# dV outer products that read 32 rows, 31 of them zero, in place of one row

## Chip, cores, metric

One core of one Trainium2 chip. The metric is the device time of one execution in microseconds. "Faster" or "slower" is said of a change of more than 2%. All runs told here are fast runs; for one core that means that no run lay over 1.5% above the fastest of its kernel.

## The reference

A decode block with its backward pass. What matters here is attention with one query per head: 32 heads, 8192 keys, head size 192, all in bf16. For each head the gradient of V is an outer product of the softmax row with the gradient of the attention output, the gradient of K one of dS with the query:

```python
scores = jnp.einsum('bhqd,bhkd->bhqk', q, k) * Dh ** (-0.5)   # q has one row
p = _softmax(scores, axis=-1)
o = jnp.einsum('bhqk,bhkd->bhqd', p, v)
# ... projection, MLP, and then jax.vjp of all of it:
# dV[k, :] = p[k] * dO[:],   dP[k] = V[k, :] . dO,   dK[k, :] = dS[k] * q[:]
```

Reading K and V and writing dK and dV is nearly all of the traffic: 342 MB read and 226 MB written.

## The kernel before

The forward half takes up to about 555 us. The backward half walks 64 steps, two per head. Each step reads one V tile of 128x6144 and writes one tile of dV and one of dK. dV is made on TensorE: for every block of keys an outer product of one row of the transposed softmax (`er`) and one row of dO. The er rows lie on partitions 0, 32, 64 and 96, and two such products, which read different blocks of rows, run side by side: the second of a pair starts 5 ns after the first (median in the trace before). ScalarE copies the result from PSUM.

```python
er_b = [bst.tile([P, R8, P], BF16, name=f"er_b{k}") for k in range(2)]
# ...
def load_er(s):
    er = er_b[s % 2]
    # ...
    nc.gpsimd.dma_start(out=er[0:P:32, :, :], in_=er_t[0][r0 : r0 + JH, :])

def mul_q(s, q):     # VectorE: V * dO, half a tile
    V_.tensor_tensor(out=pq[:, q], in0=v_l[s][...], in1=do_of(ht(s)[0])..., op=ALU.mult)

def tree_q(ps, q, lo=0, hi=DH):   # TensorE adds up the columns of it: dP
    for k in range(lo, hi, TS):
        T_.matmul(ps[:, q * JQ : (q + 1) * JQ, :], lhsT=ident_bf, rhs=pq[:, q, :, k : k + TS], ...)

def dv_groups(dV, er, doh, gs):
    for g in gs:
        m, q = divmod(g, 2)
        ps = psV.tile([P, 2, 512], FP32, name="dv_ps", tag="v")
        for k in range(2):
            for b in range(2):
                p0 = 32 * (2 * q + b)
                T_.matmul(ps[:, b, k * DH : (k + 1) * DH], lhsT=er[p0 : p0 + 1, 2 * m + k, :],
                          rhs=doh[p0 : p0 + 1, :], start=True, stop=True)
        A_.copy(out=dV4[...], in_=ps[:, :, 0:PW])
```

dO (`doh`) stands in all 128 partitions alike. The step loop mixes `mul_q`, `tree_q`, dV groups, dK products (VectorE), weight-gradient work and loads and stores (cut here). The stores and the small er loads go through one DMA queue, that of GpSimd; the V loads through SyncE's.

## Time and profile before

| | before |
|---|---|
| time, median of 3 | 1443.19 us |
| span of the profiled run | 1440.5 us |
| mean granted TensorE clock, whole / from 612 to 1384 us | 0.72 / 0.56 |
| DMA rate, 612 to 972 / 972 to 1384 us | 418 / 394 GB/s |
| one backward step, mean of steps 0 to 29 / 30 to 58 | 13.2 / 13.7 us |

The granted clock is the share of full speed that the clock records of the trace give TensorE. In the trace before these are 52 records; they hold only 0.5 and 1.0 and change only at the edges of windows of 3.413 us. A window at half clock is called cold here, one at full clock warm. A step is counted from one dP reduction on VectorE to the next. The views are read as in the prediction below: slices for where the clock is, stretches for what each half is bound by, the chain for who carries it.

### The profile page before, as it was taken

The numbers are of one execution on the slowest core, as the hardware profiler recorded it, in microseconds if no ns is written. First come the engines' busy times: TensorE is split into PE (matmuls) and PEld (weight loads), VectorE is DVE, ScalarE is ACT, GpSimd is POOL, SyncE is SP. The second block draws the span as 40 slices with busy tenths as digits, with TensorE's granted clock in tenths as the row PEclk, the third lists the DMA queues.
The fourth block names the chain that finished last, engine by engine and source line by source line (L and its number), as shares of the span: only waits on it lengthen the run. The fifth ranks groups of instructions, "written<-read, shape, count | busy, mean of one in ns | idle before, by whom it ended". The sixth has DMA issues, their size and how long they took to land.

```text
span 1440.5 us, 29990 instructions
## 1 busy us (share of the span) xinstructions
PE 1190.4 (83%) x12577; PEld 779.5 (54%) x12577; DVE 1110.3 (77%) x1396; ACT 879.3 (61%) x1920; POOL 138.6 (10%) x240
## 2 busy tenths in 40 slices
PE   3999999999999998876878788878878778778784
PEld 1677777777777677533444444444444444444442
DVE  4999999999999997776667667766667667666773
ACT  0777777677777763545656566655565556555653
POOL 0000000000000000212111111111111111111111
PEclk7999999999999997765555555555555555555655
DMA  9999999999999994699999999999999999999998
GB/s 375 401 420 418 418 415 417 401 416 407 414 411 413 418 399 176 249 413 416 424 422 417 409 420 419 417 419 413 370 425 394 417 376 407 382 398 404 382 363 364
DMA packets 77764, 570.39 MB, mean 396 GB/s; under 512 B 8606, under 2 KB 26734, under 8 KB 37566
## 3 DMA queue, kind: packets, MB, share of 16 engines
q1 hardware_dynamic: 51418, 342.02, 58.7%
q0 software_dynamic: 26192, 226.47, 38.3%
q8 instruction: 98, 1.61, 0.4%
q14 instruction: 36, 0.29, 0.0%
q10 hardware_dynamic: 20, 0.00, 0.0%
HBM read 342.00 MB, written 225.91 MB: 394 GB/s over the span
## 4 chain that ended last, share of the span: by engine, by line
PE 42%; DVE 28%; DMA 12%; issue 8%; ACT 7%; POOL 1%; SPq 0%; ACTq 0%; POOLq 0%; DVEq 0%
PE dot_ps L970 19%; DMA KB<-in_A_k_cache_dram 9%; DVE prod L303 8%; PE dv_ps L981 7%; DVE pq L961 6%; DVE prod L308 4%; PE wT_ps L857 4%; PE mp L386 4%; PE dot_ps L314 3%; DVE vs L364 2%; PE mp L391 2%; ACT wT L858 2%; ACT KB L982 2%; DMA out_dram<-KB 2%; DMA out_dram<-stg 1%
## 5 line engine op out<-in xcount | busy, mean ns | idle before, releaser
L982 ACT CAST KB<-dv_ps 128x768 bf16<-128x768 f32 x504 | 382.3, 803 | 281.6 <-PE dv_ps L981 280.7
L970 PE MATMUL dot_ps<-pq,ident_bf 128*128 128x256 bf16 x1536 | 357.7, 402 | 76.8 <-DVE pq L961 76.6
L371 ACT ACTIVATE vs<-VB,Ef 128x192 bf16<-128x192 bf16 x840 | 303.2, 443 | 0.0
L970 PEld LDWEIGHTS <-ident_bf 128*128 128x128 bf16 x1536 | 187.9, 133 | 201.5 <-issue 141.8
L981 PE MATMUL dv_ps<-do_r,er_b 1*128 1x192 bf16 x2048 | 220.2, 333 | 55.2 <-ACT KB L982 54.9
L303 DVE TENSOR_TENSOR prod<-KB,qs_bc 128x6144 bf16<-128x6144 bf16 x62 | 207.9, 3353 | 21.1 <-DMA KB<-in_A_k_cache_dram 14.0
L986 DVE TENSOR_TENSOR KB<-qs_bc,dS 128x3072 bf16<-128x3072 bf16 x126 | 220.5, 1750 | 0.1
L961 DVE TENSOR_TENSOR pq<-VB,do_r 128x3072 bf16<-128x3072 bf16 x126 | 220.5, 1750 | 0.0
L981 PEld LDWEIGHTS <-er_b 1*128 1x128 bf16 x2048 | 92.7, 111 | 173.8 <-issue 170.5
L386 PE MATMUL mp<-vs,KB 128*128 128x193 bf16 x1920 | 185.2, 249 | 0.0
L386 PEld LDWEIGHTS <-KB 128*128 128x128 bf16 x1920 | 165.4, 98 | 18.5 <-issue 6.5
L318 DVE TENSOR_REDUCE dP<-dot_ps 128x32 f32<-128x512 f32 x64 | 44.2, 691 | 149.3 <-PE dot_ps L970 149.3
L838 POOL DMA_DIRECT2D er_b<-er_t x64 | 40.9, 640 | 1144.4 <-DVE ln_xc L755 554.0
L314 PE MATMUL dot_ps<-prod,ident_bf 128*128 128x512 bf16 x372 | 96.5, 398 | 46.9 <-DVE prod L308 46.7
L364 DVE TENSOR_TENSOR vs<-VB,E 128x1728 bf16<-128x1728 bf16 x120 | 123.6, 1051 | 0.0
L308 DVE TENSOR_TENSOR prod<-prod 128x3072 bf16<-128x3072 bf16 x62 | 108.7, 1754 | 1.0
L858 ACT COPY wT<-wT_ps 128x1024 bf16<-128x1024 bf16 x84 | 80.8, 962 | 42.9 <-PE wT_ps L857 42.8
L391 PE MATMUL mp<-vs,KB 128*64 128x193 bf16 x1920 | 103.4, 251 | 0.0
L391 PEld LDWEIGHTS <-KB 128*64 128x64 bf16 x1920 | 77.3, 110 | 19.6 <-issue 19.6
L314 PEld LDWEIGHTS <-ident_bf 128*128 128x128 bf16 x372 | 38.0, 107 | 85.6 <-issue 58.3
L351 ACT ACTIVATE E<-S_h,negm 128x256 bf16<-128x256 f32 x30 | 15.2, 508 | 109.1 <-DVE negm L528 109.1
L1229 POOL DMA_DIRECT2D out_dram<-KB x127 | 68.8, 546 | 32.5 <-ACT KB L982 17.5
(338 smaller groups left out, 1011.9 us busy)
## 6 DMA issues: line engine op xcount, KB each, us to landing
out_dram<-KB POOLq DMA_DIRECT2D x125, 1536.0 KB, 12.0
VB<-in_A_v_cache_dram SPq DMA_DIRECT2D x124, 1536.0 KB, 11.3
KB<-in_A_k_cache_dram SPq DMA_DIRECT2D x63, 1536.0 KB, 12.0
wo_st<-in_A_wo_dram SPq DMA_DIRECT2D x30, 480.0 KB, 11.9
w_st<-in_A_wq_dram SPq DMA_DIRECT2D x12, 960.0 KB, 10.2
out_dram<-stg POOLq DMA_DIRECT2D x8, 960.0 KB, 14.2
out_dram<-wo_st POOLq DMA_DIRECT2D x16, 480.0 KB, 17.9
out_dram<-w_st POOLq DMA_DIRECT2D x7, 960.0 KB, 13.3
```

What stands on the lines that cost most here:

```text
L303: V_.tensor_tensor(out=prod, in0=src, in1=vec[:, None, :].to_broadcast([P, JH, DH]), op=ALU.mult)
L308: V_.tensor_tensor(out=prod[:, :, 0:w], in0=prod[:, :, 0:w], in1=prod[:, :, w : 2 * w], op=ALU.add)
L314: T_.matmul(ps, lhsT=ident_bf, rhs=prod[:, :, k : k + TS], start=(k == 0), stop=(k == w - TS))
L364: V_.tensor_tensor(out=vs[:, 0:n, 0:DH].rearrange("p j (a b) -> p j a b", b=4), in0=v[:, v0 : v0 + n, :].rearrange("p j (a b) -> p j a b", ...
L371: A_.activation(out=vs[:, k, 0:DH], in_=v[:, v0 + k, :], func=ACT.Copy, scale=Ef[:, j0 + k : j0 + k + 1])
L386: T_.matmul(mp[:, 0:MW], lhsT=kb[:, j0 + k, 0:P], rhs=vs[:, k, 0:MW], start=(q == 0 and k == 0), stop=(z and k == JQ - 1), skip_group_chec ...
L391: T_.matmul(mp[p0 : p0 + 64, MO : MO + MW], lhsT=kb[:, j0 + k, P:DH], rhs=vs[:, k, 0:MW], start=False, stop=(z and k >= JQ - 2), skip_grou ...
L961: V_.tensor_tensor(out=pq[:, q], in0=v_l[s][:, q * JQ : (q + 1) * JQ, :], in1=do_of(ht(s)[0])[:, None, :].to_broadcast([P, JQ, DH]), op=AL ...
L970: T_.matmul(ps[:, q * JQ : (q + 1) * JQ, :], lhsT=ident_bf, rhs=pq[:, q, :, k : k + TS], start=(k == 0), stop=(k == DH - TS), skip_group_c ...
L981: T_.matmul(ps[:, b, k * DH : (k + 1) * DH], lhsT=er[p0 : p0 + 1, 2 * m + k, :], rhs=doh[p0 : p0 + 1, :], start=True, stop=True)
L982: A_.copy(out=dV4[:, 2 * q : 2 * q + 2, m * PW : (m + 1) * PW], in_=ps[:, :, 0:PW])
L986: V_.tensor_tensor(out=dK[:, lo:hi, :].rearrange("p j (a b) -> p j a b", b=4), in0=qh.rearrange("p (a b) -> p a b", b=4)[:, None, :, :].to ...
```

## The change

Its intent is to let each dV product read a whole block of 32 rows. The block's other 31 er rows are made zero once, so the result stays the same; the loads only ever write partitions 0, 32, 64 and 96.

```diff
     er_b = [bst.tile([P, R8, P], BF16, name=f"er_b{k}") for k in range(2)]
+    for er in er_b:
+        nc.gpsimd.memset(er, 0.0)
...
-                    T_.matmul(..., lhsT=er[p0 : p0 + 1, 2 * m + k, :], rhs=doh[p0 : p0 + 1, :], ...)
+                    T_.matmul(..., lhsT=er[p0 : p0 + 32, 2 * m + k, :], rhs=doh[p0 : p0 + 32, :], ...)
```

## The prediction

> **What bounds the kernel now.** I read the page's first two parts first (span, busy time, the 40 slices), then the costliest groups, then the table of stretches for the second half, the chain of waits in it, and last the clock in stretches of 3.41 us.
>
> ```profile
> span 1440.5 us, 29990 instructions
> PE 1190.4 (83%) x12577; PEld 779.5 (54%) x12577; DVE 1110.3 (77%) x1396; ACT 879.3 (61%) x1920; POOL 138.6 (10%) x240
> PEclk7999999999999997765555555555555555555655
> DMA  9999999999999994699999999999999999999998
> ```
>
> The kernel has two halves. Up to about 555 us (forward) TensorE runs at its full clock. From about 576 us (backward: dV outer products, dP dot products, dK products) the granted clock is half with short exceptions, although TensorE is busy some 80% of the time there. The change touches only the backward half. What binds there is seen by cutting it in two (columns after the window: PE, PEld, DVE, ACT, POOL busy, clock, DMA share, GB/s):
>
> ```profile
> 612.00:972.00 360.00, 284.88 (x2140) 162.33 (x2137) 246.36 (x339) 210.54 (x305) 58.37 (x100) 0.58 1.01 418
> 972.00:1404.00 432.00, 349.90 (x2585) 197.32 (x2584) 294.93 (x416) 247.90 (x354) 65.64 (x111) 0.54 0.98 394
> ```
>
> The first stretch moves 418 GB/s, as much as the forward half does at its best (420 in the slices): transfers bind it. The second moves 394, so something else holds it back there. The chain of waits inside 972 to 1404 us names it:
>
> ```profile
> by line: PE dot_ps L970 36.4%; PE dv_ps L981 12.9%; DVE pq L961 11.7%; PE wT_ps L857 8.1%; issue 7.0%; ACT KB L982 3.4%; ACT wT L858 3.2%; DMA out_dram<-KB 2.4%; DVE dP L318 1.7%; ACT v_bc L1064 1.7%; DVE dq_junk L1097 1.5%; PE do_ps L871 1
> ```
>
> TensorE carries at least 57% of it (36.4 + 12.9 + 8.1), at half clock. So the late part is bound by a cold TensorE, with the transfers close behind: if it ran at 418 GB/s it would take 432 x 394/418 = 407 us. 25 us is about all that a faster TensorE can win there.
>
> The groups that matter:
>
> ```profile
> L970 PE MATMUL dot_ps<-pq,ident_bf 128*128 128x256 bf16 x1536 | 357.7, 402 | 76.8 <-DVE pq L961 76.6
> L981 PE MATMUL dv_ps<-do_r,er_b 1*128 1x192 bf16 x2048 | 220.2, 333 | 55.2 <-ACT KB L982 54.9
> ```
>
> [...]its clock records are only 0.5 and 1.0, and between 26 us and the end every change falls on a multiple of 3.413 us. [...]at 128 columns the shortest one-row load took 90 ns, the shortest 128-row load 95 ns. [...]the median one-row matmul here took 343 ns.[...]
>
> **How this trace says activity is counted.** The next two tables are the same six windows on the clock's own grid: all work, then the dV products alone (PE busy, ACT busy, clock, DMA share, GB/s).
>
> ```profile
> 879.13:882.54 3.41, 3.41 (x23) 1.69 (x21) 3.41 (x4) 0.91 (x2) 0.00 (x0) 0.50 1.01 413
> 882.54:885.96 3.42, 3.42 (x26) 2.18 (x23) 1.63 (x1) 2.84 (x4) 0.00 (x0) 0.50 1.00 419
> 885.96:889.37 3.41, 1.88 (x21) 1.20 (x20) 2.86 (x4) 2.39 (x5) 1.36 (x3) 1.00 1.00 409
> 892.78:896.20 3.42, 3.42 (x24) 1.62 (x22) 3.35 (x8) 1.37 (x3) 0.00 (x0) 0.50 0.97 402
> 896.20:899.61 3.41, 3.41 (x22) 1.71 (x20) 0.82 (x7) 2.07 (x3) 0.00 (x0) 0.50 1.02 432
> 899.61:903.02 3.41, 2.05 (x31) 1.26 (x28) 3.38 (x4) 3.15 (x5) 0.64 (x1) 1.00 1.03 437
> ```
>
> ```profile
> 879.13:882.54 3.41, 1.16 (x12) 0.91 (x2) 0.50 1.01 413
> 882.54:885.96 3.42, 0.67 (x8) 1.92 (x3) 0.50 1.00 419
> 892.78:896.20 3.42, 1.27 (x12) 1.37 (x3) 0.50 0.97 402
> 896.20:899.61 3.41, 0.76 (x10) 2.07 (x3) 0.50 1.02 432
> ```
>
> TensorE is busy all of the windows at 879, 882, 892 and 896. The two with 0.67 and 0.76 us of dV are followed by the full clock, the two with 1.16 and 1.27 us are not. So one-row products fill time without counting. I then did this for all windows: each matmul counts columns/clock x rows/128 x output columns/128, put 0.1 us after its start (the shift that sorted best). With the dV products at 1/128, in effect nothing, a cold window is followed by the full clock if the sum is at least 0.75 of the window: 228 of 231 obey. A warm window keeps the clock from about 0.36 on: 178 of 179 obey. If a one-row product counted as its whole block of 32 rows, 13 cold and 2 warm windows would disobey. And transposes, whose moving operand is the identity and so is almost all zeros, must count in full (3 disobey; 10 if they count nothing). So zeros count and rows count, as far as this trace can tell.
>
> **The change part by part.** (a) 2048 dV matmuls and their loads read 32 rows. [...]the four row blocks, the number of instructions and every engine's order stay as they were (compared instruction by instruction, only the memsets are new). Cost 0. (b) Two memsets of 128x1024 bf16 on GpSimd. The trace has 128x128 f32 in 0.20 us; eight times that is an estimate of 1.6 us each, 3.2 us. They stand ahead of the first er loads, issued at 555.67 us, whose first reader starts at 575.7; these loads landed in 1.8 to 12.8 us, which leaves slack. GpSimd idles before. Cost 0, at most 1 us. (c) The activity: each dV product now counts 32/128. Counted over the windows after 612 us, 55 of 209 cold ones reach 0.75 where 20 do now; after 972 us, 29 of 123. Of 26 warm windows 8 rather than 7 hold.
>
> What that makes of the late part: 432 us are 127 windows. Chance to rise 29/123 = 0.24, to fall about 0.65 (18 of 26 is 0.69, a little better with the higher count): share warm 0.24/(0.24 + 0.65) = 0.27, or 34 windows, where the mean clock 0.54 says 10 now. That is 24 more. I take two thirds, 16, because a warm window empties TensorE's backlog and makes the next ones thinner. The value of one: over the 29 steps of the backward loop from 981 to 1378 us, the step's length fitted against its number of transposes and its warm windows falls by 0.85 us per warm window (an estimate from scattered steps, residual 1.1 us); for the steps from 657 to 981 us it falls by 0.06, that is nothing, as a transfer-bound stretch should. So 16 x 0.85 = 14 us late, 0 early. The start of the backward half (576 to 612 us, 247 GB/s, clock 0.74) and the tail after 1404 may give 1 us each. Sum: 16 us, to 1427.
>
> **Rivals.** (i) The monitor counts switching data, or blocks of rows, not the rows read: then nothing changes but the memsets, 1443 to 1445. For it: I know only one-row and many-row cases; against it: the transposes and the 13 disobeying windows. I give it 0.2. (ii) The clock rises and hands everything to the transfers: the late part reaches 418 GB/s, 25 us won, 1418, or a few more with start and tail (1412). For it: many cold windows lie between 0.6 and 0.75; against it: a warm window does the same work in half the time, so its sum falls below the 0.36 that holds it (before: 0.20 at 899.61 us). The clock will go up and down, not stay. (iii) Vector and Scalar engine become the bound: DVE is busy 295 of 432 us and ACT 248 late, and product, tree and sum of one step follow each other; this is within the measured 0.85 us. (iv) Slower: memsets delaying the first loads[...]; nothing in the trace shows either.
>
> **Range and chances.** 0.8 x 1427 + 0.2 x 1443 is 1430; I say 1429, range 1415 to 1443.5: the lower end is the late part at full transfer rate plus a little, the upper end the change doing nothing. Faster by over 2% needs less than 1414.3, more than the transfers leave: 0.08. Slower by over 2%: 0.01.
>
> **What would show it.** In the changed profile: dV matmuls listed with 32 rows at 330 to 345 ns when cold; PEclk after 612 us up from about 0.55 to 0.60 to 0.68; windows full of dV products and trees followed by the full clock; 612 to 972 us still at about 418 GB/s and as long as before; the late part at 400 to 412 GB/s. It is wrong if the clock stays at 0.55 (rival i), if it goes above 0.75 (rival ii, hold misjudged), or if it rises and the time does not fall, which would mean that the late part waits for something else than TensorE.

Where cuts are marked, statements of the hardware were taken out that no trace of this case shows. The paragraph ahead of "How this trace says activity is counted" is measured in the trace before ("its" there means that trace). The zero of part (a): the rows read do not change a matmul's time. The traces show it: at 192 columns the cold median in the trace before is 362 ns with one row (dv_ps) and 364 ns with 128 (do_ps), the warm one 241 and 245 ns, and with 32 rows in the changed trace it is 362 and 241 ns. The profile models the ends of matmuls, so by starts alone: a group of four dV products takes 0.433 us cold up to the start of the next matmul in both traces (medians). The sum: 14 us late, 0 early, 1 us each for start and tail, 16 us in all, to 1427. "Monitor", here and in the expectations below, is a name for whatever sets the clock records; the traces show only the records. "Half the time" and the "columns/clock" of the count are in the traces as the distance between the starts of dP products of 256 columns that follow each other: 213 ns cold and 109 ns warm, 0.42 ns per column at full clock. The emptied backlog is seen in the warm windows at 885 and 899 us: 1.88 and 2.05 us of TensorE in 3.41.

## The result

1420.17 us, median of 4 runs (1417.97 to 1423.84), against 1442.90 us for the kernel before on the same chip. The ratio is 0.984, 95% interval 0.981 to 0.987. A ratio is the mean time of one kernel's fast runs over the mean of the other's fast runs of the same rounds, so it is not quite the ratio of the medians. In two later groups on the chip the same kernel gave 0.987 and 0.986. So the change wins 1.3 to 1.6%, within the 2% band, 18 to 23 us.

The page of the changed kernel (span, busy time, slices):

```profile
span 1421.7 us, 29995 instructions
PE 1125.7 (79%) x12577; PEld 747.1 (53%) x12577; DVE 1111.8 (78%) x1396; ACT 876.5 (62%) x1920; POOL 141.0 (10%) x242
PEclk9999999999999997756576657767666667676755
DMA  9999999999999995599999999999999999999998
```

The clock row from slice 18 on has 5s, 6s and 7s where it had almost only 5s. TensorE is busy 65 us less with the same 12577 matmuls. The costliest groups that answer to those of before:

```profile
L972 PE MATMUL dot_ps<-pq,ident_bf 128*128 128x256 bf16 x1536 | 332.9, 380 | 95.0 <-DVE pq L963 94.5
L983 PE MATMUL dv_ps<-do_r,er_b 32*128 32x192 bf16 x2048 | 200.7, 306 | 60.7 <-ACT KB L984 58.6
```

The dV products read 32 rows (32*128 instead of 1*128) and got faster, 306 ns instead of 333 on average. So did the dP products, which the change does not touch: 380 instead of 402. Both follow from the clock, not from the rows: after 612 us the median dV product takes, in both traces, 362 ns cold and 241 ns warm, the median dP product 421 and 273, and only the share of warm ones grew. The stretches (PE, PEld, DVE, ACT, POOL busy, clock, DMA share, GB/s):

```profile
612.00:972.00 360.00, 264.06 (x2120) 151.93 (x2118) 243.93 (x337) 207.41 (x301) 58.43 (x99) 0.65 1.01 415
972.00:1384.00 412.00, 310.88 (x2585) 179.40 (x2584) 294.66 (x416) 246.06 (x353) 65.89 (x111) 0.67 1.01 412
```

The first part had 418 GB/s and has 415; the late part had 394 and has 412. Where the 18.8 us between the two profiled runs come from is seen best by steps, since a step does the same work in both: the start up to step 0 gave 2.9 us (584.8 to 581.9), steps 0 to 29 cost 2.2 us (396.6 to 398.8), steps 30 to 58 gave 18.8 us (396.3 to 377.5), the rest cost 0.7. This is one pair of profiles. The two later profiles of the changed kernel, beside the same one before, have steps 0 to 29 at 398.9 and 392.5 us and steps 30 to 58 at 381.0 and 382.6, so the late gain is 14 to 19 us. The start lies between 578.9 and 585.6 us in all kernels, and at 581.5 in the one-row run below, so its 2.9 us are not shown to come from the change. The chain of waits from 612 to 1400 us shows what stands where TensorE was (before: PE dot_ps 32.9%, PE dv_ps 11.8%, PE wT_ps 7.3%, DMA out_dram<-KB 2.8% in the same view):

```profile
by line: PE dot_ps L972 25.8%; issue 13.3%; DMA out_dram<-KB 8.9%; DVE pq L963 8.9%; PE dv_ps L983 8.7%; DMA er_b<-er_t 6.0%; PE wT_ps L859 5.3%; DMA wo_st<-in_A_wo_dram 4.1%; ACT KB L984 3.0%; ACT wT L860 2.7%; DVE KB L988 1.7%; DVE dP L31
```

TensorE went from 52% to 40% of it, transfers from about 5% to 19% (8.9 + 6.0 + 4.1).

One window shows how the clock follows. It lies on the grid on which the clock changes. The first fence has all work in it and in the next one, the second the dV products alone (PE and ACT busy, clock, DMA share, GB/s):

```profile
1205.77:1209.19 3.42, 3.42 (x24) 1.73 (x21) 3.25 (x12) 1.72 (x4) 0.00 (x0) 0.50 0.97 405
1209.19:1212.60 3.41, 3.14 (x36) 1.92 (x33) 3.11 (x5) 3.05 (x5) 0.56 (x1) 1.00 1.08 447
```

```profile
1205.77:1209.19 3.42, 1.11 (x12) 1.72 (x4) 0.50 0.97 405
```

It is as full of dV (1.11 us) as the windows at 879 and 892 us of before, which the half clock followed. Counted as in the prediction, the other matmuls fill 0.65 of it; with the dV products at 32/128 it is 0.78, over the 0.75 fitted in the trace before, and the next window has the full clock. Windows that come to 0.73 in this trace (at 680, 769 and 1349 us among others) are not followed by it.

### The profile page after: what moved, and what is told of

Its sections match the earlier page's. It is cut to its first block, busy times and chain, and to the rows that moved or that the text cites. A ratio compares the mean times of both kernels' runs of the same rounds, so it can differ in the third digit from the quotient of the medians.

```text
span 1421.7 us, 29995 instructions
## 1 busy us (share of the span) xinstructions
PE 1125.7 (79%) x12577; PEld 747.1 (53%) x12577; DVE 1111.8 (78%) x1396; ACT 876.5 (62%) x1920; POOL 141.0 (10%) x242
## 4 chain that ended last, share of the span: by engine, by line
PE 34%; DVE 26%; DMA 21%; issue 9%; ACT 7%; POOL 2%; SPq 0%; POOLq 0%; ACTq 0%; DVEq 0%
PE dot_ps L972 15%; DMA KB<-in_A_k_cache_dram 9%; DVE prod L303 8%; DVE pq L963 5%; PE dv_ps L983 5%; DMA out_dram<-KB 5%; DVE prod L308 4%; DMA er_b<-er_t 3%; PE mp L386 3%; PE wT_ps L859 3%; PE dot_ps L314 2%; DVE vs L364 2%; DMA wo_st<-in_A_wo_dram 2%; PE mp L391 2%; ACT KB L984 2%
## 5 line engine op out<-in xcount | busy, mean ns | idle before, releaser
L972 PE MATMUL dot_ps<-pq,ident_bf 128*128 128x256 bf16 x1536 | 332.9, 380 | 95.0 <-DVE pq L963 94.5
L972 PEld LDWEIGHTS <-ident_bf 128*128 128x128 bf16 x1536 | 178.7, 127 | 205.9 <-issue 153.0
L983 PE MATMUL dv_ps<-do_r,er_b 32*128 32x192 bf16 x2048 | 200.7, 306 | 60.7 <-ACT KB L984 58.6
L988 DVE TENSOR_TENSOR KB<-qs_bc,dS 128x3072 bf16<-128x3072 bf16 x126 | 220.6, 1751 | 31.6 <-DMA out_dram<-KB 28.2
L983 PEld LDWEIGHTS <-er_b 32*128 32x128 bf16 x2048 | 85.2, 105 | 167.9 <-issue 162.8
L314 PEld LDWEIGHTS <-ident_bf 128*128 128x128 bf16 x372 | 37.8, 106 | 84.4 <-issue 57.1
```

Of the source, the lines that this page charges most:

```text
L314: T_.matmul(ps, lhsT=ident_bf, rhs=prod[:, :, k : k + TS], start=(k == 0), stop=(k == w - TS))
L988: V_.tensor_tensor(out=dK[:, lo:hi, :].rearrange("p j (a b) -> p j a b", b=4), in0=qh.rearrange("p (a b) -> p a b", b=4)[:, None, :, :].to ...
```

## Experiments

Theory A: the clock follows the sum of the rows that matmuls read, data do not matter, and the time falls through the clock alone, as far as the transfers let it. Rivals: B, the memsets or their place in the GpSimd order made the gain; C, switching data count; D, blocks of 32 rows count.

### One row, memsets kept

```diff
-    lhsT=er[p0 : p0 + 32, 2 * m + k, :], rhs=doh[p0 : p0 + 32, :]
+    lhsT=er[p0 : p0 + 1, 2 * m + k, :], rhs=doh[p0 : p0 + 1, :]
```

> The changed kernel with the dV products back at one row; the two memsets stay. Theory A (the clock's monitor counts the rows that a matmul reads): the memsets do nothing, clock after 612 us back to about 0.55, time as before (ratio to before 0.998 to 1.003). Rival B (the memsets, or the order they force on GpSimd, made the gain): ratio near 0.984.

Measured: correct, ratio 1.003 (1.000 to 1.005), clock 0.54 from 612 to 1384 us. The late part:

```profile
972.00:1384.00 412.00, 332.45 (x2473) 187.92 (x2472) 278.93 (x404) 235.74 (x337) 61.35 (x104) 0.54 0.98 395
```

B falls. The memsets take part in no gain. Their place in the timeline of the changed kernel, from the start of the backward half, shows why they cost nothing:

```profile
551.46 1.84 POOL L714 MEMSET er_b<- 128x1024 bf16 x2 [549.81 <-PE ao_ps L457]
553.73 1.38 POOL L840 DMA_DIRECT2D er_b<-er_t  x2 [0.43 <-POOL er_b L714]
```

Both together take 1.84 us after 549.8 us of idleness, and the first reader of the loads behind them starts at 573.5 us.

### 16 rows

```diff
-    lhsT=er[p0 : p0 + 32, ...], rhs=doh[p0 : p0 + 32, :]
+    lhsT=er[p0 : p0 + 16, ...], rhs=doh[p0 : p0 + 16, :]
```

> 16 rows instead of 32, 15 of them zero. If the monitor counts rows, a product counts 16/128: in the trace of before 33 of 209 cold windows after 612 us would reach 0.75 (20 with one row, 55 with 32), so a clock after 612 us of 0.58 to 0.62, between 0.55 and 0.66, and a ratio of 0.990 to 0.996. If it counts whole blocks of 32 rows as soon as more than one row is read: as with 32 rows, clock 0.66, ratio 0.984.

Measured: correct, ratio 0.992 (0.989 to 0.995), clock 0.60 from 612 to 1384 us. The late part:

```profile
972.00:1384.00 412.00, 321.92 (x2574) 184.25 (x2574) 291.68 (x415) 246.62 (x355) 66.26 (x112) 0.61 1.00 409
```

Half the rows give half the rise (0.54, 0.60, 0.66) and about half the gain. D falls. The profiled run was the fastest of the four (1420.3 us, the others 1426.0 to 1430.2), so the gain is read from the ratio and not from this profile.

### The 31 rows hold ones

```diff
-        nc.gpsimd.memset(er, 0.0)
+        nc.gpsimd.memset(er, 1.0)
```

> As the changed kernel, but the 31 other rows hold 1.0 instead of 0 (dV is wrong on purpose). Theory A (rows are counted, not data): the same clock and time as the changed kernel, ratio 0.984 within 0.004. Rival C (switching data are counted): clock above 0.70 after 612 us and a ratio nearer to 0.975.

Measured: dV wrong, ratio 0.989 (0.986 to 0.992), clock 0.65 from 612 to 1384 us; the unchanged 32-row kernel has 0.984 to 0.987 and 0.65 to 0.66. The ratio is just outside the 0.004 that was expected, on the slow side. The late part:

```profile
972.00:1384.00 412.00, 306.74 (x2535) 176.53 (x2532) 289.80 (x412) 242.72 (x350) 65.68 (x111) 0.65 1.00 407
```

31 rows of ones do not raise the clock over 31 rows of zeros, so C falls as far as the er operand goes. The other operand, dO, holds data in all rows in both runs; the correct kernel with 128 rows below tests that one.

### 128 rows

```diff
-    lhsT=er[p0 : p0 + 32, 2 * m + k, :], rhs=doh[p0 : p0 + 32, :]
+    lhsT=er[:, 2 * m + k, :], rhs=doh            # sums four er rows: dV wrong on purpose
```

> The dV products read all 128 rows (four er rows at once: dV is wrong on purpose). A product counts in full but the two row blocks no longer overlap, so a dV group takes about 0.64 us cold instead of 0.43, about 0.35 warm. Theory A: the mean load of a window in full-clock time goes from 0.31 to 0.46, above the 0.35 that holds the full clock, so the clock after 612 us is above 0.9; TensorE no longer binds, the late part runs at 415 to 420 GB/s, and the time is that of the transfers: 972 us to the end 5 to 12 us shorter than in the changed kernel, ratio 0.972 to 0.982. If transfers do not bind there, it gains more than 15 us on the changed kernel (ratio under 0.973). If the clock stays under 0.75, the count by rows is wrong, and the longer products make it slower than the changed kernel.

The times of a dV group in it are estimates, here with what the trace before has: four one-row products take 0.433 us cold, as above, and 128-row products of 192 columns (do_ps) start 160 ns apart cold and 82 ns apart warm, which is 0.64 and 0.33 us for four. That products on the same rows do not overlap is shown with 64 rows below; for 128 rows it was not shown.

Measured: ratio 0.992 (0.989 to 0.995), median 1428.7 us, clock 0.85 from 612 to 1384 us. The late part:

```profile
972.00:1384.00 412.00, 264.80 (x2523) 219.09 (x2521) 287.14 (x408) 241.78 (x347) 63.30 (x107) 0.87 1.00 407
```

The clock rose, though not above the 0.9 that was expected, but the time is 5 to 9 us worse than with 32 rows, and the late rate is 407 GB/s where 415 to 420 was expected. The expectation of the time is missed. The waits from 612 to 1400 us tell why (who waits for whom, us in all, times, longest):

```profile
DVE KB L988 <- DMA out_dram<-KB: 90.3, 26, 11.1
PEld L983 <- DMA er_b<-er_t: 42.5, 12, 8.7
PE dv_ps L983 <- DMA er_b<-er_t: 40.2, 11, 8.5
```

In the changed kernel the first of these is 28.2 us and the other two under 2 us each. The last two lines are the weight loads' and the matmuls' idle time before the same products, in nearly the same stretches: laid over each other they are 42.5 us, not the 83 us of their sum, which the expectations below go by. Compute is now ahead of the transfers. It runs into buffers whose stores have not landed, and into the small er loads: 8 KB each, but queued behind stores of 1.5 MB. Their time from issue to landing, in the kernel before, the changed one, and with 128 rows:

```profile
DMA to landing us min/median/max: 1.8/6.3/12.8
```

```profile
DMA to landing us min/median/max: 1.8/9.0/19.5
```

```profile
DMA to landing us min/median/max: 1.8/10.9/20.7
```

### The changed kernel again

Unchanged, beside the next three. 

> The changed kernel once more, on the chip of this group, so that the others have it beside them: ratio to before 0.984, at most 0.004 away, clock over the run 0.77 to 0.80.

Measured: ratio 0.987 (0.985 to 0.990), median 1423.2 us, clock over the run 0.784. As expected.

### 64 rows

```diff
-    lhsT=er[p0 : p0 + 32, 2 * m + k, :], rhs=doh[p0 : p0 + 32, :]
+    lhsT=er[64 * q : 64 * q + 64, 2 * m + k, :], rhs=doh[64 * q : 64 * q + 64, :]   # dV wrong on purpose
```

> 64 rows per dV product (two er rows at once, dV wrong on purpose); the two products of a pair now use the same rows and follow each other. If the count goes by rows, the mean load is about 0.36, just above what holds the full clock: clock after 612 us between that of 32 rows (0.66) and of 128 rows (0.85), 0.72 to 0.80. If the er loads that stand behind the stores are what 128 rows ran into, the time lies at or a little under the changed kernel's minus 0 to 5 us, and the waits of TensorE on the er loads lie between the 3 us of 32 rows and the 83 us of 128 rows.

Measured: ratio 1.010 (1.006 to 1.014), slower than the kernel before; clock 0.65. A miss in clock and in time; and TensorE waits for no er load. The groups tell what I had left out:

```profile
L983 PE MATMUL dv_ps<-do_r,er_b 64*128 64x192 bf16 x2048 | 322.9, 310 | 37.5 <-ACT KB L984 37.4
```

The dV products fill 323 us of TensorE instead of 201, because two of 64 rows that use the same rows follow each other where two of 32 rows ran side by side: four take 0.82 us cold in the timeline, instead of 0.50. While they run, two 32-row products at once read 64 rows, and one 64-row product reads 64 too. So the density of a window does not rise, the chance of the full clock does not either (clock 0.65, with 32 rows 0.65 to 0.66), and only the longer work is left. This is an account after the result; no run tests it alone. I had compared the load per window and not the density in a cold, full window. By this account what raises the clock is rows per unit of time; a product of 128 rows reads all of them, and the clock there is 0.85.

### 32 rows, er loads from the Scalar queue

```diff
-        nc.gpsimd.dma_start(out=er[0:P:32, :, :], in_=...)
+        nc.scalar.dma_start(out=er[0:P:32, :, :], in_=...)
```

> The changed kernel with the small er loads issued from the Scalar queue rather than behind the output stores in the GpSimd queue. If these loads are the new wait that eats a part of the gain (6% of the chain from 612 to 1400 us), they land in 2 to 4 us instead of 9, the chain no longer names them, and the time falls by 3 to 8 us under the changed kernel. If they wait only because everything behind them is bound by transfers anyway, the time stays within 2 us.

Measured: correct, ratio 0.988 (0.986 to 0.990), against 0.987 beside it. No gain, though from 612 to 1400 us TensorE no longer waits for an er load: the 6% that the chain gave to the er loads were not worth anything at 32 rows.

### 128 rows, er loads from the Scalar queue

The edits of the 128-row run and of the last one together. 

> 128 rows (dV wrong on purpose) with the er loads from the Scalar queue. If 128 rows was slower than 32 because TensorE stood 83 us waiting for er loads, this comes out 8 to 15 us under the 128-row run, that is at 1413 to 1420 us and at or under the changed kernel. If the Vector engine's waits for output stores (90 us there) and the transfers themselves are the cause, it stays within 4 us of the 128-row run.

Measured: ratio 0.983 (0.980 to 0.985), median 1416.7 us, clock 0.85. It is 12 us under the 128-row run. TensorE's waits for er loads fell from 83 us to 17 (from 42.5 to 9.0 with the double count taken out), and the late part has 417 GB/s:

```profile
972.00:1384.00 412.00, 273.41 (x2545) 225.54 (x2544) 291.94 (x413) 246.44 (x351) 46.06 (x80) 0.86 1.01 417
DVE KB L988 <- DMA out_dram<-KB: 92.1, 25, 6.8
```

So at 128 rows the er loads were what ate the gain; the waits for stores stayed (92.1 us), so the 12 us are not theirs. The edit moves the loads out of the store queue and their issue into ScalarE's order; the two were not tested apart. With TensorE at 0.85 of its clock, the time is only 3 to 7 us under that of the changed kernel, and 8 us under the 32-row run with the same queue (1416.7 against 1424.9 us, intervals that do not touch).

### A correct kernel with 128 rows

```diff
+    dm = bst.tile([P, 4, DH], BF16, name="dm")       # room: the unused part of another tile given back
+    def masks(s, q):                                 # its calls between the dV groups are cut here
+        for v in (2 * q, 2 * q + 1):
+            V_.tensor_scalar(out=dm[:, v, :], in0=do_of(ht(s)[0]), scalar1=ident_f[:, 32 * v : 32 * v + 1], scalar2=None, op0=ALU.mult)
-    lhsT=er[p0 : p0 + 32, 2 * m + k, :], rhs=doh[p0 : p0 + 32, :]
+    lhsT=er[:, 2 * m + k, :], rhs=dm[:, 2 * q + b, :]
```

The er loads go through the Scalar queue here too. 

> A correct kernel with 128-row dV products: the er rows stay as loaded, and dO is masked into four copies that are zero in all rows but one, two small groups of Vector operations per head, written while the other half of the four is in use; er loads from the Scalar queue. If the rows are what keeps the clock up, its clock is that of the 128-row runs (0.88 to 0.89 over the run) and its time 1414 to 1421 us, 2 to 7 us under the changed kernel beside it. If the masks cost the Vector engine as much as the clock gives, it ends within 2 us of the changed kernel.

Measured: correct, 1419.9 us median of 6 (1417.6 to 1421.1), ratio 0.984 (0.982 to 0.986), clock 0.883.

Beside it the changed kernel a third time. 

> The changed kernel on this group's chip, to set beside the masked kernel: ratio to before 0.984 to 0.988, clock 0.77 to 0.80.

Measured: 1421.8 us, ratio 0.986 (0.984 to 0.988). The two intervals overlap, and the medians are 1.9 us apart, where 2 to 7 us were expected if the masks cost little. No correct version was found that beats the changed kernel clearly.

The masked run also answers what the run with ones left open. Its dO operand is zero in 127 of 128 rows, and yet the clock is that of the 128-row run with the same queue, whose dO rows all hold data (0.883 and 0.889 over the run). So zeros count in this operand too.

### One row, er loads from the Scalar queue

The kernel before with that one edit. 

> The kernel before (one row, no memsets) with the er loads from the Scalar queue: at half clock nothing waits for these loads, so time and clock as before, ratio 0.998 to 1.003. If it were faster by over 0.5%, the better time of the 128-row run with this queue would not say anything of the clock.

In the trace before, the view of er_b lists no wait for these loads.

Measured: ratio 1.004 (1.001 to 1.007), clock 0.56 from 972 to 1384 us. If anything a little slower, just outside what was expected, so the queue alone explains nothing of the 128-row result. The loss lies in the first part: steps 0 to 29 take 406.5 us there (396.6 before) at 410 instead of 418 GB/s. Why was not looked into.

### Half of dK stored

The changed kernel, with half of each dK tile left unwritten from the third step on (dK wrong). It was run on another chip.

```diff
-        store(dK_hd, s, dK, JQ if s < 2 else 0, JH)
+        store(dK_hd, s, dK, JQ if s < 2 else 0, JH if s < 2 else JQ)
```

> The changed kernel with only half of every dK tile stored from the third step on (dK wrong on purpose): 62 stores are 768 KB smaller, 48.8 MB less, which is 117 us at 417 GB/s. If the transfers hold both parts of the backward half, the time falls by 40 us or more, until TensorE at its clock of 0.65 or the chain of Vector and TensorE binds; the rate falls well under 415 GB/s. If the changed kernel's backward half is still bound by TensorE, the time falls by under 15 us.

Measured: ratio 0.959 (0.955 to 0.963), median 1381.2 us, some 40 us less. It does not fall evenly. Steps 0 to 29 take 363.6 us instead of 392 to 399 in the three profiles of the changed kernel, steps 30 to 58 take 372.3 instead of 377 to 383:

```profile
612.00:972.00 360.00, 272.68 (x2356) 160.25 (x2355) 268.16 (x367) 227.13 (x331) 63.31 (x107) 0.70 0.99 397
972.00:1340.00 368.00, 281.14 (x2325) 162.83 (x2327) 264.01 (x380) 221.49 (x319) 60.54 (x101) 0.65 0.93 359
```

The first part is bound by transfers. In the late part of the changed kernel neither transfers nor TensorE (clock 0.65) alone is worth much more: taking away traffic wins only 5 to 10 us there, and the rate drops to 359 GB/s. And raising the clock to 0.85 wins nothing there over the changed kernel (380.6 and 382.1 us in the two 128-row kernels with the Scalar queue), and 3 to 4 us over the 32-row run with that queue (385.0). Both at once was not tried.

### All windows of all runs

The prediction's count can be made for every trace; the table has eight of them: each matmul adds columns/clock x rows/128 x output columns/128 to its window of 3.413 us, and one threshold for cold and one for warm windows is fitted. The table gives how many windows disobey, if a dV product is counted as that many rows (a delay of 50 to 150 ns after the start was fitted for each entry; worked out from the traces, not an answer of the profile):

| run | rows read | as 0 | as 16 | as 32 | as 64 | as 128 | windows |
|---|---|---|---|---|---|---|---|
| before | 1 | **4** | 10 | 14 | 24 | 39 | 410 |
| one row, memsets | 1 | **2** | 7 | 10 | 18 | 32 | 408 |
| 16 rows | 16 | 7 | **7** | 13 | 29 | 54 | 401 |
| changed kernel | 32 | 10 | 5 | **3** | 16 | 53 | 401 |
| the same, ones | 32 | 12 | 7 | **5** | 20 | 54 | 401 |
| 64 rows | 64 | 17 | 15 | 13 | **11** | 48 | 417 |
| 128 rows | 128 | 37 | 32 | 29 | 19 | **5** | 398 |
| 128 rows, Scalar queue | 128 | 41 | 38 | 32 | 21 | **0** | 395 |

Every run is told best by the rows that it reads (16 is a tie, 64 nearly one), at thresholds of 0.74 to 0.77 for cold and 0.35 to 0.37 for warm windows. The thresholds are fits in the same data, but they come out alike in all runs. A recount with nothing fitted, at the prediction's 0.75, 0.36 and 0.1 us, leaves 2 to 9 windows of some 400 that disobey in each of the fourteen traces. In the masked kernel, which the table leaves out, 3 of 407 disobey when its products count as 128 rows, 81 when they count as 32.

## Why the prediction was right, and where it was off

- **Result.** 1429 was predicted, 1420 measured, inside the range of 1415 to 1443.5; a gain of 14 us was named and 18 to 23 came; "within 2%" was the likeliest case and came.
- **What binds** was right: transfers in the first part of the backward half, a cold TensorE in the late part. In the profile of the result steps 0 to 29 did not get shorter with a clock of 0.66 instead of 0.59, and steps 30 to 58 did; over three profiles the first got 2 us longer to 4 us shorter, the others 14 to 19 us shorter. The run with half of dK stored shows that transfers bind the first part.
- **The count by rows, zeros included,** was right. One row, 16, 32 and 128 rows give a clock of 0.54, 0.60, 0.65 and 0.85 from 612 to 1384 us, the data give nothing, in either operand. The clock goes up and down, as said, and 0.66 is in the stated 0.60 to 0.68.
- **Memsets and matmul times** were right: 0 each. The memsets took 1.84 us, less than the estimate of 3.2. One reading behind the matmul times was not: the "343 ns" is the median of cold and warm products together. Cold ones alone take 362 ns, with one row and with 32, and the sign "330 to 345 ns when cold" did not come. That the rows do not change the time, on which the step rests, is what the traces show (362 ns cold and 241 ns warm with both).
- **The term that was mis-sized** is "24 more. I take two thirds, 16", times "0.85 us per warm window". In the profiled run the late part had 0.67 as its mean clock, that is 41 warm windows of 121, not 26: 31 more than the 10 of before. The cut to two thirds was wrong: of the cold windows from 972 to 1404 us, 25 in 83 still reached 0.75, 0.30 and not less than the 0.24 that I had counted. The value was too high: 18.8 us over 31 windows is 0.6 us each, and 0.5 to 0.6 in the two later profiles. 31 x 0.6 in place of 16 x 0.85 makes 19 us of 14. The two errors pull opposite ways, and that they partly cancel is luck. The 0.85 was weak from the start: the same fit, redone, has a standard error of about 0.4, gives 0.46 in the one-row run with memsets, and comes out with the wrong sign in the changed kernel's trace.
- **Rival (ii)** named the time better than its clock: with 32 rows the clock fell back as the main line said, and yet the late part came to 412 GB/s, most of what the transfers allow. Had the clock stayed up, as it does at 128 rows, the time would have been only 3 to 8 us less.
- **Not foreseen** was the er load in the store queue. It entered the chain of the changed kernel with 6%, without cost there, and cost 12 us at 128 rows.

## What to carry to other kernels

In this kernel a TensorE that was busy 3.41 of 3.41 us (at 879 us) stayed at half clock, with 1.16 us of it spent on products of one row. So look at the granted clock before counting matmul time, and, where no other row block is disturbed, try padding the rows with zeros: 32 rows in place of one raised the clock from 0.56 to 0.66 here (612 to 1384 us) and won 1.3 to 1.6%. Take whole blocks of 32, not 64, if the padding would make products that ran side by side follow each other: with 64 rows a cold group of four took 0.82 us instead of 0.50, and the ratio was 1.010. Before pushing further, look how far the transfers behind allow it (from 0.65 to 0.85 of the clock won 3 to 8 us here, and that only with the er loads in the Scalar queue), and which small loads stand in a queue behind large stores (12 us at 128 rows).
